# V of the first two batches loaded as two times 72 rows of four tokens, in a fused attention and two-layer feed-forward kernel

## The chip, the cores and the metric

The program runs on one core of one Trainium2 chip. The metric is the device time of one execution in microseconds (us), as the median of several runs. A core has five engines with queues of their own: TensorE (PE, with its weight loads shown apart as PEld), VectorE (DVE), ScalarE (ACT), GpSimd (POOL) and SyncE (SP, which here issues the transfers).

## The reference

`q`, `k`, `v` are (4 batches, 8 heads, 576 tokens, 64). The attention output is the sum of two parts. The *pooled* part averages q, k and v over groups of four tokens (576 becomes 144), does a plain softmax attention on these 144 tokens and repeats each result four times. The *local* part is softmax attention within a band of seven tokens. Both are added, heads and width make 512 columns, 4 x 576 = 2304 rows, and two feed-forward layers follow:

```python
out = out_up + out_local              # (4, 8, 576, 64) -> x (2304, 512)
h = x @ w_in;  g = h * sigmoid(h);  x = g @ w_out        # 512 -> 2048 -> 512
h = x @ w_in2; r = max(h, 0);       out = (s*r*r + b) @ w_out2
```

## The kernel before

**Layers.** Rows are handled in blocks of 512 columns (four blocks, then one of 256). A block of x is kept transposed, 4 tiles of 128 x 512. Each factor of the feed-forward products is split into a high and a low part in a fast format, so that a product is three matmuls (`product`, line 820: high by high, low, and high again with the other half). `mix1` (line 830) goes over 16 slices of the inner width: 4 x 3 matmuls into `hp`, SiLU and a split on ACT and DVE, 4 x 3 matmuls into the four `y` tiles. The second layer does the same from line 930 on. The weights are split on DVE and ACT by `weights` (line 366), at most six slices ahead (`AHEAD`).

**Attention.** Batches 0 and 1 (`NBAND = 2`) do the local part on TensorE (`banded`, line 751); batches 2 and 3 do it on DVE (`local`, line 454). The pooled part is `down` (line 605) for all four; it handles a pair of heads at a time, four pairs a batch. For batches 0 and 1 its inputs come from `rows` (line 565) and `b_turn` (line 698); for batches 2 and 3 from `natural` (line 550).

**V in batches 0 and 1 before the change.** `rows` loads the first 512 tokens of a pair of heads in one transfer into a tile of 128 partitions, each with four consecutive tokens of both heads (line 575). The last 64 tokens of all eight heads come once per batch in a transfer of their own (`zv`, line 583). `pool_rows` (line 592) adds the four tokens of each partition in two DVE steps (lines 595 and 596). `pool_ends` (line 585) sums the last 64 tokens in groups of four with a matmul by a matrix of ones (`pz`, line 589) and copies the 16 rows back. In `down` the 144 pooled tokens are therefore cut in 128 and 16 (`cuts`, line 608): the turned weights `at` are made in these two pieces (line 662) and the value product `pU` (line 680) multiplies, for each head, a piece of 128 rows and then one of 16 rows. Batches 2 and 3 load V as two halves of 72 rows and cut at 72.

**What sets the order.** The kernel is written as a list of operations with a rank (`pr`), estimated costs in microseconds and the buffers that they need. `Weave.plan` (line 121) runs through that list as a simulation: at each step it takes the operation that can start first on any engine, the lowest rank deciding, and writes the instructions out in that order. It also chooses between ACT and DVE for operations marked `EITHER`, and where TensorE would stand idle ahead of the first products it puts in idle matmuls (`spin`, lines 242 and 243). Attention operations on TensorE carry costs multiplied by `slow(ps)` (line 258): 1.25 in batch 0, 1.1 later. Products have rank 100 and above, so any attention operation that is ready goes ahead of them. The plan's estimates set the order only; on the chip each engine takes its instructions in that fixed order and waits where data is late.

Of the kernel before, what the change touches and what calls it, by code (L numbers as in the profile page):

```python
# [16 lines left out]
P = 128  # L17
# [2 lines left out]
SUB = 3  # L20
HALO = 3
WIN = 7
NBAND = 2
NB = 512
GROUPS = [(6, 6, 6), (5, 5, 4, 4)]
GS = 6
QP = 72
# [8 lines left out]
HOLD = {'exp': 0.064, 'silu': 0.785}  # L36
BIAS = 0.306
START = 0.56
FLIGHT = 4
NW = 35  # L40
NACT, NACTV = 0, 1
# [36 lines left out]
class Weave:  # L78
# [42 lines left out]
    def plan(self, pr):  # L121

        ops = self.ops
        need = [len(o[3]) for o in ops]
        ready = [0.0] * len(ops)
        cand, free = {}, {}
        moved, table = 0.0, None
        flight = {"sp": [0.0] * FLIGHT, "act": [0.0] * FLIGHT}
        turns = {k: list(v) for k, v in self.turns.items()}
        slot_of, left, busy, at = {}, {}, set(), {}  # L130
        order, begin, finish, used, placed = [], [0.0] * len(ops), [0.0] * len(ops), [None] * len(ops), [()] * len(ops)

        def avail(bufs):
            t, got = 0.0, []
            for b in bufs:
                if b.slot is None and b not in slot_of:
                    if b.kind in turns and turns[b.kind][0] is not b:
                        return 1e30, got
                    s = min((s for s in self.kinds[b.kind] if s not in busy and all(s is not g for _, g in got)),
                            key=lambda s: at.get(s, 0.0), default=None)  # L140
                    if s is None:
                        return 1e30, got
                    got.append((b, s))
                    t = max(t, at.get(s, 0.0))
            return t, got

        for i, o in enumerate(ops):
            for b in o[4]:
                left[b] = left.get(b, 0) + 1
            for e in o[0]:  # L150
                cand.setdefault(e, [])
                free.setdefault(e, START)
                if not need[i]:
                    cand[e].append(i)
        for _ in ops:
            best = None
            for e, c in cand.items():
                starts = []
                for i in c:
                    t = max(ready[i], free[e])  # L160
                    if e in flight and isinstance(ops[i][1], tuple) and len(ops[i][0]) == 1:
                        t = max(t, flight[e][-FLIGHT] + 0.1)
                    if len(ops[i][0]) > 1:
                        ends = {o: max(ready[i], free[o]) + c for o, c in zip(ops[i][0], ops[i][1])}
                        if (e == "act") != (ends["act"] <= ends["dve"] + BIAS):
                            continue
                    if ops[i][6] and ops[i][6] != table:
                        t = max(t, ready[i] + HOLD[ops[i][6]])
                    t = max(t, avail(ops[i][4])[0])
                    starts.append((t, i))  # L170
                if starts:
                    t0 = min(starts)[0]
                    pick = min((pr[i], i) for t, i in starts if t <= t0 + 1e-9)
                    if best is None or t0 < best[0]:
                        best = (t0, pick[1], e)
            t, i, eng = best
            if t >= 1e30:
                raise RuntimeError("no slot: " + ", ".join(sorted({b.kind for c in cand.values() for j in c for b in ops[j][4] if b.slot is None and b not in slot_of})))
            engs, cost, _, _, bufs, _, need_table = ops[i]
            if len(engs) > 1:  # L180
                cost = cost[engs.index(eng)]
            if need_table and need_table != table:
                table = need_table
                cost += SWITCH
            placed[i] = avail(bufs)[1]
            for b, s in placed[i]:
                slot_of[b] = s
                busy.add(s)
                if b.kind in turns:
                    turns[b.kind].pop(0)  # L190
            order.append(i)
            begin[i], used[i] = t, eng
            if eng in flight and isinstance(cost, tuple):
                parts, move = cost[:2]
                for _ in range(parts):
                    t = max([t, flight[eng][-FLIGHT] + 0.1]) + (cost[2] if len(cost) > 2 else 0.47)
                    moved = max(t + 0.65, moved) + move / parts
                    flight[eng].append(moved)
                free[eng] = t
                end = moved + 0.93  # L200
            else:
                end = free[eng] = t + cost
            finish[i] = end
            for e in engs:
                cand[e].remove(i)
            for j in self.succ[i]:
                need[j] -= 1
                ready[j] = max(ready[j], end + self.lag(eng, ops[j][0]))
                if not need[j]:
                    for e in ops[j][0]:  # L210
                        cand[e].append(j)
            for b in bufs:
                left[b] -= 1
                s = slot_of.get(b, b.slot)
                at[s] = max(at.get(s, 0.0), end + 0.13)
                if not left[b]:
                    busy.discard(s)
        return order, begin, finish, used, placed
# [31 lines left out]
def dve(n, c=1):  # L250
    return c * 0.07 + n / 960.0
# [4 lines left out]


def slow(ps):
    return 1.25 if ps == "ps_first" else 1.1


def pe(n):
    return n / 2400.0 + 0.0134
# [3 lines left out]
def kernel(ctx, tc, q, k, v, w1_in, w1_out, w2_in, w2_out, s2, b2, cst, out):  # L267
# [297 lines left out]
    def rows(b, i, names, pr, kind, after=[], by="sp"):  # L565


        for nm in names:
            t = nat[b, i, nm] = Buf(kind, [P, 2, NT4, D] if nm == "v" else [P, NT4, 2 * D], F32, "n" + nm)

            def load(t=t, nm=nm):
                queue = nc.scalar if by == "act" else nc.sync
                row = (b * H + 2 * i) * S
                if nm == "v":
                    dma(t[:].rearrange("p a r d -> p a (r d)"), bass.AP(tens[nm].tensor, row * D, [[NT4 * D, P], [S * D, 2], [1, NT4 * D]]), queue)
                    return
                for a in range(2):
                    dma(t[:, :, a * D:(a + 1) * D], bass.AP(tens[nm].tensor, (row + a * S) * D, [[D, P], [P * D, NT4], [1, D]]), queue)

            op(by, (1, 0.9, 0.5) if nm == "v" else (2, 1.55, 0.73), load, w=[t], r=after, pr=pr)  # L580
            if (b, nm) not in ends_of:
                z = ends_of[b, nm] = Buf(kind, [NZ, H, D], F32, "z" + nm)
                op("sp", (1, 0.8, 0.73), lambda z=z, nm=nm: dma(z[:], tens[nm][b, :, NT4 * P:, :].rearrange("h s d -> s h d")), w=[z], r=after, pr=pr)
# [8 lines left out]
    def pool_rows(b, i, pr):  # L592

        t = nat[b, i, "v"]
        op("dve", dve(4 * D), lambda: nc.vector.tensor_tensor(out=t[:, :, 0:2], in0=t[:, :, 0:2], in1=t[:, :, 2:4], op=ALU.add), w=[t], pr=pr)
        op("dve", dve(2 * D), lambda: nc.vector.tensor_tensor(out=t[:, :, 0], in0=t[:, :, 0], in1=t[:, :, 1], op=ALU.add), w=[t], pr=pr)

# [7 lines left out]
    def down(b, i, pr, ps="ps"):  # L605
        qd, kd = q_diag[i % 2], Buf("dk", [P, SD], F32, "dk")
        plain = (b, i) in bq
        cuts = [(0, P), (P, SD)] if plain else [(0, QP), (QP, SD)]
        if plain:
            pool_rows(b, i, pr)  # L610
            (q_, qi), (k_, ki) = bq[b, i], bk[b, i]
# [58 lines left out]
            op(EITHER, (act(2 * SD), dve(2 * SD)), lambda eng, kt=kt, pT=pT, n=k1 - k0: copy(eng, at[:n, kt], pT[:]), w=[(at, kt)], r=[pT], pr=pr)  # L670
        up = upT[b]
        pU = Buf(ps, [P, SD], F32, "pU")
        for a in range(2):
            def value(a=a):
                for kt, (k0, k1) in enumerate(cuts):
                    if plain:
                        rows = nat[b, i, "v"][:, a, 0] if kt == 0 else ends_of[b, "v"][:NZ // 4, 2 * i + a]
                    else:
                        rows = sums["v"](kt)[:, a * D:(a + 1) * D]
                    nc.tensor.matmul(pU[a * D:(a + 1) * D], lhsT=rows, rhs=at[:k1 - k0, kt, :, a * DQ:(a + 1) * DQ], start=(kt == 0), stop=(kt == 1))  # L680

            op("pe", 0.33 * slow(ps), value, w=[(pU, a), (up, i)], r=[at, nat[b, i, "v"]] + ([ends_of[b, "v"]] if plain else []), pr=pr)

        def keep(eng):
            if plain:
# [134 lines left out]
    def product(t, n, lhs, rhs, w, r, first, last, pr):  # L820
# [2 lines left out]
            for i in range(3):  # L823
                nc.tensor.matmul(t(), lhsT=lhs(i), rhs=rhs(i), start=(first and i == 0), stop=(last and i == 2))  # L824

        op("pe", 3 * pe(n), fn, w=w, r=r, pr=pr)

    HP, LP = 100.0, 101.0

# [44 lines left out]
        weights(1, 0, DECF, [], RAWF) if m == 0 else weights(1, m, DEC0 + DECS * m, [split_end[1, m - AHEAD]] if m >= AHEAD else [], RAW0 + RATE * m)  # L874
    for hq in A:
        b_turn(0, hq, PT0 + PTS * hq, "ps_first")
        if hq == 0:
            pool_ends(0, PN0, "ps_first")
        down(0, hq, PN0 + PNS * hq, "ps_first")
        for js in runs(first):  # L880
# [10 lines left out]
    for b in range(1, NBAND):  # L891
        lead, rest = list(range(c1 // QB)), list(range(c1 // QB, NJ))
        vr = None
        for hq in A:
            rows(b, hq, "qkv", NAT1 + PT1S * hq, "w", [split_end[1, D1 + D1S * hq]])
            vw = v_load(b, [hq], lead, NAT1 + PT1S * hq, [split_end[1, D1 + D1S * hq]])
            b_turn(b, hq, PT1 + PT1S * hq, "ps")
            if hq == 0:
                pool_ends(b, PT1, "ps")
            down(b, hq, PT1 + PT1S * hq)  # L900
            for js in runs(lead):
# [125 lines left out]
```

## Time and profile before

| what | value |
|---|---|
| median of 3 runs | 928.7 us (928.09 to 930.0) |
| time of the profiled execution | 928.93 us |
| its span, first to last instruction | 927.1 us |
| PE busy | 907.8 us (98%) |
| DVE busy | 594.9 us (64%) |
| ACT busy | 413.7 us (45%) |
| mean granted TensorE clock | 0.993 |

The span and the 1.8 us around it make up the profiled execution. Matmuls are pipelined, and the end of each is modelled; how long a group of them keeps the engine is read from the start of the group to the start of what follows, not from its length in the row.

### The profile page before, as it was taken

How to read it: one execution, taken by the hardware profiler on the slowest of the kernel's cores; microseconds unless marked ns; L12 is line 12 of the kernel's file. 1: busy time of each engine (PE TensorE's matmuls, PEld its weight loads, DVE VectorE, ACT ScalarE, POOL GpSimd, SP SyncE). 2: the span in 40 equal slices, each digit the busy share in tenths (PEclk: the TensorE clock that was granted, in tenths of full speed). 3: DMA queues.
4: the chain of work that ended last, by engine and by line, in shares of the span. 5: the costliest groups of instructions: out<-in, count | busy, mean ns of one | idle time of the engine just before them, and what ended most of it. 6: DMA issues, size and time to landing. Idle time of an engine off the chain costs nothing.

```text
span 927.1 us, 13217 instructions
## 1 busy us (share of the span) xinstructions
PE 907.8 (98%) x5065; PEld 738.9 (80%) x5065; DVE 594.9 (64%) x1137; ACT 413.7 (45%) x911; POOL 0.2 (0%) x4
## 2 busy tenths in 40 slices
PE   8889999999999999999999999999999999999997
PEld 6667777777777877777889988888888888888896
DVE  4999599689999999995139998332232224222332
ACT  4966778667357433342234543332232224222322
POOL 0000000000000000000000000000000000000000
PEclk7999999999999999999999999999999999999999
DMA  9995411445333212220068460020011000100101
GB/s 197 276 270 174 137 46 46 126 122 128 86 111 81 79 65 66 68 74 1 1 208 288 164 227 0 1 91 1 1 46 46 1 1 23 45 1 1 29 18 24
DMA packets 98331, 78.10 MB, mean 84 GB/s; under 512 B 62557, under 2 KB 84443, under 8 KB 98267
## 3 DMA queue, kind: packets, MB, share of 16 engines
q1 hardware_dynamic: 97078, 76.95, 28.7%
q8 instruction: 40, 0.66, 0.3%
q10 hardware_dynamic: 1188, 0.30, 0.2%
q14 instruction: 25, 0.20, 0.1%
HBM read 67.79 MB, written 9.44 MB: 83 GB/s over the span
## 4 chain that ended last, share of the span: by engine, by line
PE 75%; DVE 16%; ACT 4%; DMA 2%; issue 1%; SPq 0%; ACTq 0%; DVEq 0%
PE hp L824 34%; PE o L824 21%; PE y L824 14%; DVE tmp L500 3%; DVE tmp L463 2%; DVE sc L466 2%; DVE tmp L505 2%; DVE gl L845 2%; DVE tmp L506 1%; PE pU L680 1%; PE pS L644 1%; PE pB L765 1%; PE pBO L807 1%; DVE pv L507 1%; DMA zk<-in_k_dram 1%
## 5 line engine op out<-in xcount | busy, mean ns | idle before, releaser
L824 PE MATMUL hp<-xh,wi 128*128 128x512 f32 (+1 forms) x640 | 205.2, 380 | 2.5 <-ACT g L843 2.0
L824 PE MATMUL y<-gh,wo 128*128 128x512 f32 (+1 forms) x640 | 200.7, 376 | 0.0
L824 PE MATMUL hp<-yh,wi 128*128 128x512 f32 (+1 forms) x640 | 185.9, 368 | 0.0
L824 PE MATMUL o<-wo,gh 128*128 128x512 f32 x576 | 177.4, 389 | 0.0
L956 DVE SCALAR_TENSOR_TENSOR gl<-r,sbt,gh 128x512 fp32r<-128x512 f32 (+1 forms) x80 | 55.8, 698 | 151.0 <-ACT gh L954 150.7
L824 PEld LDWEIGHTS hp<-xh,wi 128*128 128x128 f32 x640 | 116.9, 189 | 27.3 <-ACT g L843 5.7
L824 PEld LDWEIGHTS y<-gh,wo 128*128 128x128 f32 x640 | 116.9, 189 | 20.6 <-issue 1.2
L824 PEld LDWEIGHTS hp<-yh,wi 128*128 128x128 f32 x640 | 116.5, 189 | 20.2
L954 ACT ACTIVATE gh<-r,sbt 128x512 fp32r<-128x512 f32 (+1 forms) x80 | 54.6, 683 | 159.5 <-PE o L824 151.1
L824 PEld LDWEIGHTS o<-wo,gh 128*128 128x128 f32 x576 | 107.8, 188 | 22.1
L824 PE MATMUL y<-gl,wo 128*128 128x512 f32 (+1 forms) x320 | 118.3, 370 | 0.0
L824 PE MATMUL hp<-xl,wi 128*128 128x512 f32 (+1 forms) x320 | 118.2, 369 | 0.0
L824 PE MATMUL hp<-yl,wi 128*128 128x512 f32 (+1 forms) x320 | 117.7, 368 | 0.0
L824 PE MATMUL o<-wo,gl 128*128 128x512 f32 x288 | 112.0, 389 | 0.0
L844 ACT CAST gh<-g 128x512 fp32r<-128x512 f32 (+1 forms) x80 | 46.2, 577 | 102.1 <-PE y L824 101.3
L952 DVE SCALAR_TENSOR_TENSOR r<-r,sbt 128x512 f32<-128x512 f32 (+1 forms) x80 | 55.8, 697 | 51.3 <-ACT r L951 51.2
L845 DVE TENSOR_TENSOR gl<-g,gh 128x512 fp32r<-128x512 f32 (+1 forms) x80 | 50.6, 632 | 39.9 <-ACT gh L844 39.5
L951 ACT ACTIVATE r<-hp 128x512 f32<-128x512 f32 (+1 forms) x80 | 44.5, 556 | 63.9 <-DVE gl L956 45.4
L824 PEld LDWEIGHTS hp<-yl,wi 128*128 128x128 f32 x320 | 60.3, 188 | 10.0
L824 PEld LDWEIGHTS y<-gl,wo 128*128 128x128 f32 x320 | 60.5, 189 | 9.3 <-DVE gl L845 0.7
L824 PEld LDWEIGHTS hp<-xl,wi 128*128 128x128 f32 x320 | 60.5, 189 | 7.6
L843 ACT ACTIVATE g<-hp 128x512 f32<-128x512 f32 (+1 forms) x80 | 44.4, 556 | 48.1 <-DVE gl L845 45.2
(134 smaller groups left out, 1007.7 us busy)
## 6 DMA issues: line engine op xcount, KB each, us to landing
wi_raw<-in_moe_w_in_dram SPq DMA_DIRECT2D x32, 512.0 KB
wo_raw<-in_moe_w_out_dram SPq DMA_DIRECT2D x32, 512.0 KB
yd<-ys SPq DMA_DIRECT2D x16, 256.0 KB
yt<-yd SPq DMA_DIRECT2D x4, 1024.0 KB
nq<-in_q_dram SPq DMA_DIRECT2D x16, 144.0 KB
nk<-in_k_dram SPq DMA_DIRECT2D x16, 144.0 KB
lk<-in_k_dram SPq DMA_DIRECT2D x6, 384.0 KB
lv<-in_v_dram SPq DMA_DIRECT2D x6, 384.0 KB
```

The lines of the kernel that those rows point to most:

```text
L463: op("dve", dve(n * WIN * D), lambda t=t, i0=i0, n=n, h2=h2: nc.vector.tensor_tensor(out=t[:], in0=wide(qs[:, h2, i0:i0 + n, :].unsqueeze( ...
L466: op("dve", dve(n * WIN * D), lambda t=t, i0=i0, n=n, h2=h2: nc.vector.tensor_reduce(out=sc[:, h2, i0:i0 + n, :], in_=t[:], axis=AX.X, op= ...
L500: op("dve", dve(n * WIN * D), lambda t=t, i0=i0, n=n, h2=h2: nc.vector.tensor_tensor(out=t[:], in0=wide(e[:, h2 * ns + i0:h2 * ns + i0 + n ...
L505: nc.vector.tensor_tensor(out=t[:, :, 0:3], in0=t[:, :, 0:3], in1=t[:, :, 4:7], op=ALU.add)
L824: nc.tensor.matmul(t(), lhsT=lhs(i), rhs=rhs(i), start=(first and i == 0), stop=(last and i == 2))
L843: op("act", act(n), lambda g=g, hp=hp: nc.scalar.activation(out=g[:], in_=hp[:], func=AF.Silu), w=[g], r=[hp], pr=-5, table="silu")
L844: op("act", act(n), lambda g=g, gh=gh: nc.scalar.copy(out=gh[:], in_=g[:]), w=[gh], r=[g], pr=-5)
L845: op("dve", dve(n), lambda g=g, gh=gh, gl=gl: nc.vector.tensor_tensor(out=gl[:], in0=g[:], in1=gh[:].bitcast(F32), op=ALU.subtract), w=[gl ...
L951: op("act", act(n), lambda r=r, hp=hp: nc.scalar.activation(out=r[:], in_=hp[:], func=AF.Relu), w=[r], r=[hp], pr=-5)
L952: op("dve", dve(n) + 0.07, lambda r=r: nc.vector.scalar_tensor_tensor(out=r[:], in0=r[:], scalar=sbt[:, 0:1], in1=r[:], op0=ALU.mult, op1= ...
L954: op("act", act(n) + 0.1, lambda r=r, gh=gh: nc.scalar.activation(out=gh[:], in_=r[:], func=AF.Identity, bias=sbt[:, 1:2]), w=[gh], r=[r, ...
L956: op("dve", dve(n) + 0.07, lambda r=r, gh=gh, gl=gl: nc.vector.scalar_tensor_tensor(out=gl[:], in0=r[:], scalar=sbt[:, 1:2], in1=gh[:].bit ...
```

## The change

`VQ`, the set of batches that keep the old layout of V, is empty. V of batches 0 and 1 is loaded as two halves of 72 partitions with four tokens each, in two transfers per pair of heads; `zv`, `pz` and its copy are gone, and so is the cut at 128. The pooled sums of a pair now have 72 partitions with twice as many elements. The value product multiplies 72 rows twice. In the plan, attention operations on TensorE outside batch 0 are no longer stretched by 1.1, and each change between products and other work on TensorE costs 0.07 us (`TURN`).

```diff
+VQ = ()
+TURN = 0.07
...
-        moved, table = 0.0, None
+        moved, table, mixing = 0.0, None, False
...
-                    if ops[i][6] and ops[i][6] != table:
+                    if ops[i][6] in HOLD and ops[i][6] != table:
...
-            if need_table and need_table != table:
+            if eng == "act" and need_table and need_table != table:
...
             else:
+                if eng == "pe" and (need_table == "mix") != mixing:
+                    mixing = not mixing
+                    cost += TURN
                 end = free[eng] = t + cost
...
 def slow(ps):
-    return 1.25 if ps == "ps_first" else 1.1
+    return 1.25 if ps == "ps_first" else 1.0
...
         for nm in names:
+            if nm == "v" and b not in VQ:
+                t = nat[b, i, nm] = Buf(kind, [QP, 2, 2, 4, D], F32, "n" + nm)
+
+                def halves(t=t):
+                    for k in range(2):
+                        dma(t[:, k].rearrange("p a r d -> p a (r d)"), bass.AP(tens["v"].tensor, ((b * H + 2 * i) * S + k * 4 * QP) * D, [[4 * D, QP], [S * D, 2], [1, 4 * D]]),
+                            nc.scalar if by == "act" else nc.sync)
+
+                op(by, (2, 1.3, 0.4), halves, w=[t], r=after, pr=pr)
+                continue
...
         t = nat[b, i, "v"]
+        if b not in VQ:
+            op("dve", dve(8 * D), lambda: nc.vector.tensor_tensor(out=t[:, :, :, 0:2], in0=t[:, :, :, 0:2], in1=t[:, :, :, 2:4], op=ALU.add), w=[t], pr=pr)
+            op("dve", dve(4 * D), lambda: nc.vector.tensor_tensor(out=t[:, :, :, 0], in0=t[:, :, :, 0], in1=t[:, :, :, 1], op=ALU.add), w=[t], pr=pr)
+            return
...
-        cuts = [(0, P), (P, SD)] if plain else [(0, QP), (QP, SD)]
+        cuts = [(0, P), (P, SD)] if plain and b in VQ else [(0, QP), (QP, SD)]
...
+        ends = plain and b in VQ
+
+        def value(pairs):
+            for kt, a in pairs:
+                k0, k1 = cuts[kt]
+                if not plain:
+                    rows = sums["v"](kt)[:, a * D:(a + 1) * D]
+                elif not ends:
+                    rows = nat[b, i, "v"][:, kt, a, 0]
+                else:
+                    rows = nat[b, i, "v"][:, a, 0] if kt == 0 else ends_of[b, "v"][:NZ // 4, 2 * i + a]
+                nc.tensor.matmul(pU[a * D:(a + 1) * D], lhsT=rows, rhs=at[:k1 - k0, kt, :, a * DQ:(a + 1) * DQ], start=(kt == 0), stop=(kt == 1))
...
+            for a in range(2):
+                op("pe", 0.33 * slow(ps), partial(value, [(0, a), (1, a)]), w=[(pU, a), (up, i)], r=[at, nat[b, i, "v"]], pr=pr)
...
-        op("pe", 3 * pe(n), fn, w=w, r=r, pr=pr)
+        op("pe", 3 * pe(n), fn, w=w, r=r, pr=pr, table="mix")
...
-        if hq == 0:
+        if hq == 0 and 0 in VQ:
             pool_ends(0, PN0, "ps_first")
...
-            if hq == 0:
+            if hq == 0 and b in VQ:
                 pool_ends(b, PT1, "ps")
```

## Rows read from the trace of the kernel before

**Rows 1.** Busy time by stretch: us, PE, PEld, DVE, ACT, POOL, PEclk, DMA share, GB/s.

```profile
0.00:20.00 20.00, 15.95 (x197) 13.07 (x198) 8.38 (x23) 7.79 (x31) 0.20 (x4) 0.74 1.01 194
20.00:62.00 42.00, 36.52 (x456) 26.81 (x453) 41.35 (x114) 34.39 (x129) 0.00 (x0) 1.00 1.05 288
62.00:200.00 138.00, 137.74 (x909) 102.55 (x907) 114.19 (x287) 102.90 (x258) 0.00 (x0) 1.00 0.42 114
200.00:480.00 280.00, 276.70 (x1307) 220.37 (x1302) 231.86 (x391) 119.75 (x235) 0.00 (x0) 1.00 0.26 74
```

**Rows 2.** Timeline of PE, value products of one pair in batch 1 (start, length).

```profile
105.94 0.46 PE L680 MATMUL pU<-dat,nv 128*64 128x144 f32 x2
106.33 0.45 PE L680 MATMUL pU<-dat,zv 16*64 16x144 f32 x2
...
107.48 0.50 PE L824 MATMUL y<-gh,wo 128*128 128x512 f32 x1
```

**Rows 3.** Timeline of PE, value products of two pairs in batches 2 and 3.

```profile
221.76 0.86 PE L680 MATMUL pU<-dat,nv 72*64 72x144 f32 x8
222.55 0.98 PE L644 MATMUL pS<-dk,q_diag 128*96 128x144 f32 x6
...
234.53 0.72 PE L680 MATMUL pU<-dat,nv 72*64 72x144 f32 x8
235.17 0.50 PE L824 MATMUL hp<-xh,wi 128*128 128x512 f32 x1
```

**Rows 4.** Timeline of PE around the sum of the last tokens in batch 1.

```profile
75.01 0.40 PE L824 MATMUL y<-gl,wo 128*128 128x512 f32 x1
75.24 0.40 PE L824 MATMUL y<-gh,wo 128*128 128x512 f32 x1
75.57 1.03 PE L589 MATMUL pz<-zv,four 64*16 64x512 f32 x2
76.53 0.50 PE L824 MATMUL y<-gh,wo 128*128 128x512 f32 x1
76.87 0.40 PE L824 MATMUL y<-gl,wo 128*128 128x512 f32 x1
```

**Rows 5.** DVE sums of V by line: durations in ns min/median/max, first and last start.

```profile
L595 DVE TENSOR_TENSOR nv<-nv x8: 391/414/426, 12.3 to 155.7; 128x256 f32<-128x256 f32 x8
L596 DVE TENSOR_TENSOR nv<-nv x8: 275/280/285, 13.3 to 156.6; 128x128 f32<-128x128 f32 x8
L601 DVE TENSOR_TENSOR nv<-nv x8: 677/679/687, 187.8 to 297.0; 72x512 f32<-72x512 f32 x8
L602 DVE TENSOR_TENSOR nv<-nv x8: 357/412/420, 188.5 to 299.1; 72x256 f32<-72x256 f32 x8
```

**Rows 6.** Chain that ended last, up to 62 us (start, us, what).

```profile
14.12 1.81 PE pz L589 x2
...
41.20 0.60 DVE wo L394
...
51.61 1.55 PE pU L680 x8
...
61.30 0.74 PE hp L824 x2
```

**Rows 7.** Timeline of DVE in the first 20 us, with the idle time before and its releaser.

```profile
12.26 0.42 DVE L595 TENSOR_TENSOR nv<-nv 128x256 f32<-128x256 f32 x1 [2.74 <-DMA nv<-in_v_dram]
...
15.97 0.68 DVE L318 COPY zv<-pz 16x512 f32<-16x512 f32 x1 [0.43 <-PE pz L589]
```

**Rows 8.** Busy time by stretch of 1 us, columns as in rows 1.

```profile
18.00:19.00 1.00, 1.00 (x6) 0.99 (x6) 1.00 (x4) 0.00 (x0) 0.00 (x0) 0.50 1.18 287
19.00:20.00 1.00, 1.00 (x35) 0.94 (x34) 1.00 (x6) 0.74 (x2) 0.00 (x0) 0.98 1.08 203
```

**Rows 9.** Timeline of SP's queue, the transfers of V of the first pair.

```profile
5.78 0.82 SPq L331 DMA_DIRECT2D nv<-in_v_dram  x1
7.05 0.61 SPq L331 DMA_DIRECT2D zv<-in_v_dram  x1
```

More of the change, by code (lines that the diff above doesn't have):

```diff
@@ L672, in down @@
         pU = Buf(ps, [P, SD], F32, "pU")
[L673 to L682, printed above, removed]
+        ends = plain and b in VQ
[9 more added lines that the diff above has]
+                nc.tensor.matmul(pU[a * D:(a + 1) * D], lhsT=rows, rhs=at[:k1 - k0, kt, :, a * DQ:(a + 1) * DQ], start=(kt == 0), stop=(kt == 1))
+        if ends:
+            op("pe", 1.2 * slow(ps), partial(value, [(0, 0), (0, 1), (1, 0), (1, 1)]), w=[pU, (up, i)], r=[at, nat[b, i, "v"], ends_of[b, "v"]], pr=pr)
+        else:
+            for a in range(2):
+                op("pe", 0.33 * slow(ps), partial(value, [(0, a), (1, a)]), w=[(pU, a), (up, i)], r=[at, nat[b, i, "v"]], pr=pr)
         def keep(eng):
```

## The prediction

> **What bounds the kernel now.** I read the busy time by stretch first, then the timeline of TensorE where the edited operations run, the chain that ended last in the opening stretch, and at last the timelines of VectorE and of SP's queue. The first view splits the run [rows 1]. Up to 20 us the kernel waits for its first transfers: PE is busy 15.95 us (idle matmuls included), DVE only 8.38. From 20 to 62 us DVE has no time left (41.35 of 42) and PE has (36.52 of 42): batch 0's attention and the first weight splits share DVE. From 62 us on PE decides: busy 137.74 of 138 and then 276.70 of 280, so all its idle time up to 480 us is 0.26 + 3.30 = 3.6 us. There a microsecond of PE work removed is a microsecond of time; before 62 us it need not be. After 480 us the second layer runs, which the edits don't touch.
>
> **Value products, batch 1.** Four matmuls (two passes each) make `pU` of a pair. With 128 and 16 rows they start at 105.94 and the next work at 107.48 [rows 2]: 1.54 us. The alternation is dear: the 16-row product starts 0.39 us after the 128-row one. The three other pairs of batch 1 show the same steps. Batches 2 and 3 do the same product with 72 rows twice, in 235.17 - 234.53 = 0.64 us, once in 222.55 - 221.76 = 0.79 [rows 3]. The changed kernel issues just that form, so 0.75 to 0.90 us go per pair; I take 0.90, as three of the four pairs that I looked at in batches 2 and 3 take 0.64 or 0.65. Four pairs: -3.6 us (bounds -3.0 to -3.6), all on PE while it is the bound.
>
> **The sum of the last tokens, batch 1.** `pz` holds PE from 75.57 to 76.53, 0.96 us. It is a visit between products as well: those follow one another by 0.23 us (75.01 to 75.24), but 0.33 pass up to `pz` and 0.34 after the first product behind it [rows 4], so a visit costs 0.10 + 0.11 more. Together -1.17 us; should the plan put other attention work into that place, the 0.21 stays: bounds -0.96 to -1.17. Its copy there runs on ACT, which has slack (102.90 of 138) [rows 1]; nothing for it.
>
> **The sums of V on DVE.** Before, a pair costs 414 + 280 ns; as 72 rows with twice the elements 679 + 412 ns [rows 5]. That is +0.40 us a pair, for eight pairs +3.2 us. In batch 1 the cover is DVE's slack, 114.19 of 138 [rows 1]: nothing, at worst +1.6 if that slack is gone when the pair is due. In batch 0 there is no cover after 20 us.
> The row shows more elements per partition in place of more partitions, and the time following the elements. The Trainium skill's page "Trainium Kernel Development and Optimization", under Best Practices, says to tile to 128 partitions always; that speaks against this edit. By it, with all 3.2 us on the path, the sum below would end at about 925.1 in place of 923.5.
>
> **The opening, batch 0.** Four terms. (a) `pz` takes 1.81 us on the chain at 14.12 [rows 6], at half the clock, and DVE waits 0.43 us for it and copies for 0.68 [rows 7]. With both gone the next transposes of PE and DVE's work come forward; as ACT's exponentials of the first pair are late next, I take DVE's part, -1.1 us (bounds 0 to -1.8). (b) The first pair's longer sum, +0.40, ahead of the first band mask: its data was already what DVE waited for (2.74 us) [rows 7]. (c) The other three pairs' sums on a full DVE: +1.2. (d) Value products 0.90 cheaper in four pairs: one of these groups lies on the chain, at 51.61 [rows 6]; -0.9 for it, the rest is hidden behind DVE (bound -3.6). Sum: -1.1 + 0.4 + 1.2 - 0.9 = -0.4 us, with bounds of -1.8 - 3.6 = -5.4 (DVE's additions covered by weight splits that nobody waits for yet) and 0.4 + 1.2 = +1.6.
>
> **Transfers.** Per pair two transfers of V in place of one, and no `zv`: SP issues 8 more and 2 fewer. One issue holds SP for 0.82 or 0.61 us in the opening [rows 9]. For the first pair the second half takes about the place of `zv`, so whatever is queued behind stays where it was; the bytes are the same in all. Later pairs push what is behind them in SP's queue (q and k of the next pair, weights) back by one issue each, at most 0.8 us; PE waits for none of these after 62 us. Zero, bounds 0 to +0.8 on the way to the first product. The cut at 72 changes the rows of the turned weights, not their number or their columns: zero.
>
> **The new plan.** `TURN` and the factor of 1.0 change no instruction, but every start time that the plan computes, hence the order on all engines and the choice of ACT or DVE. No row shows the result. Best case: the waits after 62 us vanish, -3.6; as bound above I take the same amount again, +3.6 [rows 1]. A visit counted with its real cost should put waits in the right place, reshuffled ranks may do the opposite: zero.
>
> **Sum.** -3.6 - 1.2 - 0.4 + 0 = -5.2 us. Against the profiled execution, 928.93 us (span 927.1 and 1.8 around it), that is 923.7; this execution lies 0.2 above the median, so the median becomes **923.5 us**.
>
> **Rivals.**
> *The opening gains in full* (0.16). The chain in the opening changes engine many times, and DVE's time between 20 and 62 us is partly weight splits that PE needs much later; if the plan puts the sums in front of these, the -5.4 of the opening is had in place of -0.4: 918.5. Against it: DVE's stretch is as good as full [rows 1].
> *The new order gives most of it back* (0.13). After 62 us the waits double by 3.6: 923.5 + 3.6 = 927.1. For it: the fixed ranks stay as they were while every computed time moves. Against it: waits are few today and the costs of the plan come nearer to the rows (0.33 us per half of a value product is what rows 3 show).
> *DVE sets the opening, slower* (0.13). Place: DVE's queue between 20 and 62 us. The longer sums, planned ahead of x's last pieces, let the plan move weight splits in front of attention work. A split of a tile has three steps of 0.60 (lines 387, 390 and 394; one stands in [rows 6]), 1.8 us. PE then starts its unbroken products later, and that is never regained. Beyond 5.2 / 1.8 = 2.9 tiles the gain is eaten; four tiles give 923.5 + 7.2 = 930.7. For it: 41.35 of 42. Against it: the work added there is only 1.6 us, less the 0.68 of the copy. The rule on 128 partitions cited above points the same way.
> *The dear step isn't due to the 16 rows* (0.03). Were it the alternation of the two heads' output halves, it would stay: only `pz` and the opening would count, 928.7 - 1.2 - 0.4 = 927.1. Against it: the 72-row groups alternate these halves as well [rows 3].
> *The clock rises late* (0.03). TensorE runs at 0.50 through 18 to 19 us and at full rate (2.4 GHz) from 19 to 20 on, after a stretch with PE busy [rows 8]. Without `pz` PE may stand idle ahead of it. Half of the time spent at the low level is lost, so it takes some 14 us more at 0.50 to lose 7: 930.5.
>
> **How the numbers follow.** The forecast itself has 0.52, with 921.5 to 926 as its own range. A measurement of this kernel tells 0.2%, about 1.9 us, from no change: below 926.8 is faster, above 930.6 slower. Faster: 0.52 + 0.16 + 0.04 (a mild form of the second rival) = 0.72. Same: 0.09 of the second rival, 0.02 of the third, 0.03 of the fourth = 0.14. Slower: 0.11 of the third, 0.03 of the last = 0.14. The range 918.5 to 930 leaves out half of the first rival (0.08), half of the third (0.06) and the last (0.03).
>
> **What would show it.** Right: `pU` groups of batch 1 that last 0.64 to 0.80 us from start to next start, no `pz`, sums of V on DVE at 0.68 and 0.41, the unbroken products, which begin at 61.30 on the chain [rows 6], within a microsecond of that, and the stretch from there to the second layer some 4.8 us shorter. Wrong: an unbroken stream that starts more than 2 us later (third rival) or 3 us earlier (first), PE idle time beyond 6 us between 62 and 480 (second), steps of 0.39 in `pU` (fourth), or 0.50 in the clock column after 20 us (last).

## The result, and the profile after

The changed kernel takes 934.47 us (median of 4 runs, 933.07 to 936.11), the kernel before 928.39 beside it: a ratio of 1.0065 [1.005, 1.0081], 6.1 us slower. Forecast were 923.5 us and a range up to 930. The profiled execution, the fastest of the four, took 933.07 us (span 931.1, PE busy 907.2, DVE 598.9, ACT 402.6, mean clock 0.995), 4.1 more than the one of before.

Busy time by stretch, changed kernel, columns as in [rows 1]:

```profile
0.00:20.00 20.00, 16.91 (x280) 15.33 (x282) 10.91 (x31) 9.78 (x40) 0.20 (x4) 0.91 1.05 205
20.00:62.00 42.00, 36.69 (x490) 27.86 (x486) 41.69 (x110) 31.39 (x111) 0.00 (x0) 1.00 1.07 287
62.00:200.00 138.00, 134.02 (x893) 99.94 (x894) 121.77 (x298) 93.03 (x239) 0.00 (x0) 0.99 0.43 117
200.00:480.00 280.00, 275.01 (x1292) 218.85 (x1291) 222.26 (x385) 119.61 (x228) 0.00 (x0) 1.00 0.23 67
```

The reader is to see PE's third and fourth row: idle time is now 3.98 + 4.99 = 9.0 us, where it was 3.6 [rows 1]. At the same time ACT lost 9.9 us of work between 62 and 200 us and DVE gained 7.6: the plan also shares the copies out differently.

The value products of a pair in batch 1, timeline of PE, changed kernel:

```profile
107.04 0.40 PE L851 MATMUL y<-gh,wo 128*128 128x512 f32 x1
107.36 0.72 PE L703 MATMUL pU<-dat,nv 72*64 72x144 f32 x8
108.01 0.98 PE L663 MATMUL pS<-dk,q_diag 128*96 128x144 f32 x6
108.73 0.49 PE L851 MATMUL y<-gh,wo 128*128 128x512 f32 x1
```

The group, four matmuls of two passes each, keeps PE for 108.01 - 107.36 = 0.65 us; it was 1.54 [rows 2]. No `pz` is left. The sums of V on DVE, by line (ns min/median/max, first and last start), cost what 72 rows cost in the other batches [rows 5], and the first one starts 1.0 us sooner than before [rows 7]:

```profile
L611 DVE TENSOR_TENSOR nv<-nv x8: 657/681/689, 11.3 to 151.6; 72x512 f32<-72x512 f32 x8
...
L612 DVE TENSOR_TENSOR nv<-nv x8: 395/414/421, 12.4 to 152.9; 72x256 f32<-72x256 f32 x8
```

So the work went, and the time came back, about half of it as waits. What PE waits for between 62 and 480 us, first in the kernel before (us in total, times, longest), then the longest in the changed one. `pt` turns the local results `pv` of batches 2 and 3, `g` is SiLU's result, `gl` its low part, `dat` the turned weights of `pU`, `dk` the pooled keys:

```profile
PE pt L515 <- DVE pv L507: 2.0, 6, 0.6
PE pt L515 <- DVE sm L489: 0.6, 1, 0.6
PE hp L824 <- ACT g L843: 0.3, 1, 0.3
...
```

```profile
PE hp L851 <- ACT g L870: 2.7, 3, 2.0
PE pt L520 <- DVE pv L512: 2.1, 5, 0.9
PE pU L703 <- ACT dat L323: 1.0, 3, 0.5
PE y L851 <- DVE gl L872: 0.8, 2, 0.6
PE pS L663 <- DVE dk L634: 0.4, 1, 0.4
...
```

In all that view has 3.3 us in 10 waits before and 8.7 us in 21 waits after, on many tiles and none of them large except one. That one ends the opening. The chain that ended last shows who was late there (start, us, what; L389 and L399 are steps of a weight split), and the busy time by 1 us what followed:

```profile
60.69 0.68 DVE wo L399
61.37 0.14 DVE be L800
61.51 0.33 DVE f L389
61.84 0.17 DVE wi L399
62.01 0.35 issue
62.37 0.69 DVE gl L872
...
63.14 0.61 ACT g L870
...
63.79 0.50 PE hp L851
```

```profile
64.00:65.00 1.00, 1.00 (x5) 0.82 (x5) 1.00 (x2) 0.78 (x2) 0.00 (x0) 0.98 0.90 146
65.00:66.00 1.00, 1.00 (x4) 0.71 (x4) 1.00 (x3) 0.84 (x2) 0.00 (x0) 0.50 0.93 158
66.00:67.00 1.00, 1.00 (x4) 0.81 (x3) 1.00 (x3) 0.00 (x0) 0.00 (x0) 0.50 1.09 184
67.00:68.00 1.00, 1.00 (x4) 0.81 (x3) 1.00 (x4) 0.95 (x2) 0.00 (x0) 0.50 1.15 263
68.00:69.00 1.00, 1.00 (x5) 0.79 (x5) 1.00 (x3) 0.99 (x2) 0.00 (x0) 0.81 1.01 208
```

PE stood idle for 2.03 us ahead of 63.79, and from 65.0 on its clock was granted at 0.50 (1.2 of 2.4 GHz) for 3.4 us: the clock column adds up to 0.02 + 3 x 0.50 + 0.19 = 1.7 us lost.

**The account of the 9.3 us between forecast (-5.2) and profile (+4.1).** From the start of each PE instruction to the next, idle time apart: the opening ends at 63.79 in place of 61.30 [rows 6], but 36 product matmuls stand before that point, not 24; at 0.23 us each that is 2.49 - 2.76 = -0.3, near the -0.4 forecast. From there to the last `y` matmul of the first layer (528.88 before, 531.33 after) PE takes 467.5 us both times, where -4.8 from the layout and -2.8 for the products already done would have left 460.0. The 7.5 us are 3.8 of idle time, 1.7 of the clock, 1.4 of longer steps at the attention's matmuls (those of the banded local part `pBT`, `pB` and `pBO` +1.7, the others together -0.3) and 0.6 in the products. The last 1.5 us come in the second layer, 0.45 of it idle time (0.3 a wait on `gl`), the rest mostly three product matmuls more that stand behind the last `y`. That is 0.1 + 7.5 + 1.5 = 9.1; the 0.2 left are rounding and the time around the span.

### The profile page after: what moved, and what is told of

Read it like the earlier page. It is cut to its first block, busy times and chain, and to the rows that moved or that the text cites. A ratio compares the mean times of both kernels' runs of the same rounds, so it can differ in the third digit from the quotient of the medians.

```text
span 931.1 us, 13426 instructions
## 1 busy us (share of the span) xinstructions
PE 907.2 (97%) x5171; PEld 740.4 (80%) x5171; DVE 598.9 (64%) x1153; ACT 402.6 (43%) x878; POOL 0.2 (0%) x4
## 4 chain that ended last, share of the span: by engine, by line
PE 64%; DVE 24%; DMA 4%; ACT 4%; issue 3%; SPq 1%; DVEq 0%; ACTq 0%
PE hp L851 30%; PE o L851 20%; PE y L851 11%; DVE tmp L505 3%; DVE tmp L468 3%; DVE sc L471 3%; DVE gl L872 2%; DMA vw<-in_v_dram 2%; DVE tmp L510 2%; SPq L336 1%; DVE tmp L511 1%; DVE f L392 1%; DMA yd<-ys 1%; DVE f L395 1%; DMA nq<-in_q_dram 1%
```

## The experiments

The theory: the layout brings what was forecast, and the plan's new costs lose more than that, by putting PE's work in an order that waits. The rivals: the layout is itself slower (the opening, DVE's longer sums), or the clock is what was lost; later on, that the charge hurts by its place, by the length that it gives the plan, or by leaving no slack for late data.

Two numbers of the plan were changed with the layout: the **charge** at each change between products and other work (`TURN`), and the **factor** on attention's costs on PE outside batch 0. Medians are in us; the kernel before took 928.4 to 929.05 beside them. PE's idle time is 415.5 less its busy time in the stretch 64.5 to 480 us, so that the wait at the end of the opening is not in it.

| kernel | V | charge | factor | median (runs) | ratio to before | PE idle |
|---|---|---|---|---|---|---|
| before | old | 0 | 1.1 | 928.39 | 1 | 3.6 |
| after | new | 0.07 | 1.0 | 934.47 (4) | 1.0065 [1.005, 1.0081] | 7.2 |
| order_kept | new | order of before | | 929.04 (12) | 1.0001 [0.999, 1.0011] | 5.9 |
| kept_warm | new | order of before | | 928.25 (11) | 0.9998 [0.9988, 1.0008] | 6.1 |
| v_only | new | 0 | 1.1 | 927.02 (11) | 0.998 [0.9971, 0.9989] | 5.3 |
| plan_only | old | 0.07 | 1.0 | 935.17 (5) | 1.0066 [1.0054, 1.0078] | 7.1 |
| b1_only | new in batch 1 | 0.07 | 1.0 | 938.29 (4) | 1.0096 [1.0083, 1.0109] | 9.8 |
| v_turn | new | 0.07 | 1.1 | 935.62 (5) | 1.0078 [1.0066, 1.009] | 8.0 |
| v_half | new | 0.035 | 1.0 | 925.02 (5) | 0.9959 [0.9946, 0.9972] | 5.9 |
| v_slow | new | 0 | 1.0 | 923.58 (5) | 0.9949 [0.9937, 0.9961] | 3.2 |
| v_fast | new | 0 | 0.8 | 924.35 (11) | 0.9962 [0.9951, 0.9972] | 3.5 |
| v_att | new | 0 | 1.3 | 932.63 (7) | 1.0037 [1.0023, 1.0051] | 8.9 |
| slow_only | old | 0 | 1.0 | 928.68 (11) | 0.9999 [0.9989, 1.0009] | 3.6 |
| after_lag | new | 0.07 | 1.0 | 935.63 (6) | 1.008 [1.0057, 1.0103] | 8.5 |
| vslow_lag | new | 0 | 1.0 | 923.81 (5) | 0.995 [0.9937, 0.9962] | 2.0 |
| turn_even | new | 0.07, products cheaper | 1.0 | 923.11 (5) | 0.9944 [0.993, 0.9957] | 2.9 |
| all_slow | new | 0.07, DVE and ACT dearer | 1.0 | 923.01 (5) | 0.9936 [0.9924, 0.9949] | 4.0 |

### Layout and plan taken apart

**order_kept** is the kernel before with V in the new layout. The operations for the last tokens stay in the plan and issue nothing, so every engine keeps its order of before; nothing of the result is left out.

```diff
...
-        op("pe", 1.0, lambda: nc.tensor.matmul(pz[:], lhsT=four1[:NZ], rhs=z[:].rearrange("p h d -> p (h d)")), w=[pz], r=[z, four1], pr=pr)
+        op("pe", 1.0, lambda: None, w=[pz], r=[z, four1], pr=pr)
...
-        cuts = [(0, P), (P, SD)] if plain else [(0, QP), (QP, SD)]
+        cuts = [(0, QP), (QP, SD)]
...
-                        rows = nat[b, i, "v"][:, a, 0] if kt == 0 else ends_of[b, "v"][:NZ // 4, 2 * i + a]
+                        rows = nat[b, i, "v"][:, kt, a, 0]
```

> The new V layout (two halves of 72 rows, no last-token sum, value products of 72 rows) with the order of before: the plan sees the costs and buffers of before, and the operations of the last tokens stay in it with nothing to issue. Theory A (the instructions save what the prediction said, the new order of the plan loses it): 921 to 925 us, value products of batch 1 at 0.64 to 0.80 us a pair, idle time of TensorE between 62 and 480 us near the 3.6 of before. Rival B (the longer sums on VectorE and the extra transfers cost it, wherever they stand): 930 to 936 us, with the unbroken products starting later than 61.3 us.

**v_only** is the changed kernel with both numbers of the plan as before, **plan_only** the kernel before with both new numbers, **b1_only** the changed kernel with the old layout in batch 0.

```diff
-TURN = 0.07
+TURN = 0.0
...
-    return 1.25 if ps == "ps_first" else 1.0
+    return 1.25 if ps == "ps_first" else 1.1
```

> The new V layout, planned with the costs of before (no cost for a change of kind, attention work stretched by 1.1). Theory A1 (any new order loses, since the ranks are fixed): 930 to 936 us. Theory A2 (the new costs in the plan are at fault): 921 to 926 us. Rival B (the layout itself): 932 to 937 us.

```diff
+TURN = 0.07
...
+                if eng == "pe" and (need_table == "mix") != mixing:
+                    mixing = not mixing
+                    cost += TURN
...
-    return 1.25 if ps == "ps_first" else 1.1
+    return 1.25 if ps == "ps_first" else 1.0
...
```

> The V layout of before, planned with the cost of 0.07 us for a change of kind and the factor of 1.0. Theory A1 (any new order loses): 930 to 937 us. Theory A2 (the new costs are at fault): 934 to 940 us, about 6 us plus the 5 that the layout saves above before. Rival B (the layout itself): 927 to 930 us, as before.

```diff
-VQ = ()
+VQ = (0,)
```

> The changed kernel with the old V layout in batch 0 alone (there the four value products of a pair stand in one operation, those of 128 rows first). If the loss is made in batch 0's opening: 924 to 929 us. If it is made by the order of the mixed stretch after 62 us: 931 to 937 us.

The two numbers of the plan, on the layout of before, cost 0.66% or 6.3 us by themselves (plan_only), as much as the whole change. The layout without them gains only 1.9 us (v_only), with both of them 0.7 (the changed kernel less plan_only), and in the order of before nothing (order_kept). b1_only is the slowest of all, though its batch 1 has the cheap value products: what moves these times is the order, and its loss can't be read as a price of batch 0's layout. Only plan_only fell where a theory put it, and it fell into the ranges of two: order_kept and v_only lie in none of their ranges, and b1_only lies 1.3 us above its second one.

Its windows show in part why order_kept gains nothing. Busy time of order_kept between 30 and 60 us, columns as in [rows 1]:

```profile
32.00:33.00 1.00, 0.41 (x3) 0.32 (x4) 1.00 (x5) 0.89 (x3) 0.00 (x0) 1.00 1.13 230
33.00:43.00 10.00, 10.00 (x80) 8.00 (x81) 9.60 (x29) 8.39 (x35) 0.00 (x0) 0.51 1.09 254
...
53.00:60.00 7.00, 7.00 (x50) 5.00 (x50) 5.60 (x12) 2.06 (x5) 0.00 (x0) 0.54 1.08 341
```

PE is busy for 0.41 of the microsecond from 32 to 33, and then works at half the clock, 17 us in all; 19 product matmuls are begun by 62 us, where before had 27. After that PE waits 5.6 us in 13 waits, where before waits 3.3. Eight product matmuls at 0.23 us and 2.3 us more of waits are 4.1 of the 4.8 us that the layout was to bring. **kept_warm** is order_kept with idle matmuls where batch 0 lost its work, to part these two.

```diff
...
-        op("pe", 1.0, lambda: None, w=[pz], r=[z, four1], pr=pr)
+        op("pe", 1.0, lambda: fill(30) if ps == "ps_first" else None, w=[pz], r=[z, four1], pr=pr)
...
+                if ps == "ps_first":
+                    fill(10)
```

> The kernel with the new V layout in the order of before, and idle matmuls on TensorE in the opening, 30 in the place of the first batch's sum of last tokens and 10 after each head's value product, about as long as what the layout took away there. If the gain of the layout was lost because TensorE had less to do in the opening and its clock fell to 0.50 for 17 us: no fall between 25 and 62 us, some 27 products started by 62 us as before, and 926 to 928 us against 929.0 without them. If the clock is not the reason: 928.5 to 930.5 us.

Its profile shows one fall of the clock, 3.4 us long, and 24 product matmuls by 62 us, but the time is only 0.8 us lower than order_kept's and the intervals overlap; 928.25 lies between the two ranges that were expected. The clock in the opening is at most a small part; the waits stayed (7.3 us in 15). turn_even (below) says the same: its clock is 0.53 from 39 to 50 us, where v_slow's is 1.00, and it is as fast as v_slow.

### Which of the two numbers

**v_turn** puts the factor back to 1.1, **v_slow** takes the charge away, **v_fast** also sets the factor to 0.8, **v_half** halves the charge.

```diff
-    return 1.25 if ps == "ps_first" else 1.0
+    return 1.25 if ps == "ps_first" else 1.1
```

> The new V layout with one of the two new plan costs: 0.07 us for a change of kind, attention work still stretched by 1.1. Theory C (a plan that takes TensorE for slower than its rows say puts TensorE's operations where the results of VectorE and ScalarE come just in time, and TensorE waits; a plan that takes it for faster leaves slack): this is the slowest TensorE of all plans, so 934 to 939 us, idle time of TensorE between 62 and 480 us 7 us or more. Rival D (each new order lands anywhere, no trend): 926 to 937 us, no relation to the others.

```diff
-TURN = 0.07
+TURN = 0.0
```

> The new V layout with the other new plan cost: no cost for a change of kind, attention work stretched by 1.0 in place of 1.1. Theory C: TensorE is taken for faster than in the plan that gave 927.0, so 924 to 927.5 us. If the factor of 1.0 is the culprit: 931 to 935 us. Rival D: 926 to 937 us.

```diff
-TURN = 0.07
+TURN = 0.0
...
-    return 1.25 if ps == "ps_first" else 1.0
+    return 1.25 if ps == "ps_first" else 0.8
```

> The new V layout, no cost for a change of kind, attention work of the later batches shrunk to 0.8 in the plan, well under its rows. Theory C: 922 to 926.5 us, idle time of TensorE between 62 and 480 us under 5 us. Rival E (a plan nearer to the rows is better, and the changed plan lost for another reason): 930 us or more. Rival D: 926 to 937 us.

```diff
-TURN = 0.07
+TURN = 0.035
```

> The changed kernel with half the cost for a change of kind, 0.035 us; its plan ends at 915.4 us of its own count, between those that gave 923.6 (908.6) and 934.5 (923.9). Theory C, and rival F as well: 926 to 931 us. Rival D (no trend, each order by luck): outside of that, most likely over 931 or under 926.

Taking the charge out is enough to undo the loss: without it the changed kernel takes 923.58 us, the forecast's 923.5 and 0.4 under the range expected. Half of the charge costs 1.4 us, the whole of it 10.9; v_half's 925.02 lies under 926, where it was said to speak for the rival that each order lands by luck: the loss does not grow evenly with the charge. v_slow between 62 and 480 us, busy time of two stretches and what PE waited for:

```profile
62.00:200.00 138.00, 136.84 (x923) 104.18 (x923) 123.37 (x303) 92.34 (x245) 0.00 (x0) 1.00 0.44 119
200.00:480.00 280.00, 277.49 (x1329) 223.17 (x1328) 226.64 (x387) 124.61 (x238) 0.00 (x0) 1.00 0.27 78
```

```profile
PE pt L520 <- DVE pv L512: 0.8, 4, 0.3
PE hp L851 <- ACT g L870: 0.8, 1, 0.8
PE y L851 <- DVE gl L872: 0.7, 1, 0.7
PE pt L520 <- DVE sm L494: 0.4, 1, 0.4
...
```

Idle time is 1.16 + 2.51 = 3.7 us, as before the change; `pt` waits 1.2 us in place of 2.3 and no `pU` waits. Its last `y` of the first layer starts at 521.94, the changed kernel's 9.4 us later, and by the account of PE's steps over the whole time up to it these 9.4 are 4.0 of idle time, 3.7 in the products (1.7 of it the clock) and 1.7 at attention's own steps.

### What the charge does: its place, its length, or PE's pace

Charging 0.07 us at each change is not wrong as a price: in the kernel before, a step from a product into other work takes 0.289 us against 0.236 between products. So why does it hurt? **v_att** makes PE slow in the plan without any charge, by the factor alone. **slow_only** sets the factor to 1.0 on the old layout, to have the layout by itself at the plan costs of v_slow.

```diff
-TURN = 0.07
+TURN = 0.0
...
-    return 1.25 if ps == "ps_first" else 1.0
+    return 1.25 if ps == "ps_first" else 1.3
```

> The new V layout, no cost for a change of kind, attention work of the later batches stretched by 1.3 in the plan: the plan ends at 924.4 us of its own count, as the changed kernel's does (923.9), without any charge at a change. Theory C (what loses is a plan that takes TensorE for slow, whatever makes it slow): 932 to 937 us. Rival F (the charge at the changes is what loses): 923 to 928 us, as with factors of 0.8 to 1.1.

```diff
-    return 1.25 if ps == "ps_first" else 1.1
+    return 1.25 if ps == "ps_first" else 1.0
```

> The V layout of before, no cost for a change of kind, attention work at 1.0 in place of 1.1. Beside the 923.6 us of the new layout with the same plan costs this prices the layout: if it is worth the 4.8 us predicted after 62 us and nothing in the opening, 927.5 to 929.5 us; if it is worth only the 1.9 us that it gave at a factor of 1.1, 924.5 to 926.5 us.

Stretching attention does much the same as the charge (932.63 us, 8.9 us idle): the place where the plan loses PE's time is not what matters. And at these plan costs the layout is worth 928.68 - 923.58 = 5.1 us, or 4.6 by the two ratios: the size that was forecast for it. That holds at this pair of numbers only; at the others the layout brought 1.9, 0.7 and 0 us (above), so how much of it is kept depends on the order.

**after_lag** and **vslow_lag** count the results of other engines 0.4 us later for PE, from 62 us of the plan on, so that no order rests on data that is ready just in time.

```diff
-                ready[j] = max(ready[j], end + self.lag(eng, ops[j][0]))
+                ready[j] = max(ready[j], end + self.lag(eng, ops[j][0]) + (0.4 if end > 62.0 and eng != "pe" and ops[j][0] == ("pe",) else 0.0))
```

> The changed kernel with both new plan costs, and one more edit in the plan: from 62 us of its own count on, a result of another engine counts as ready for TensorE 0.4 us later, so the plan puts TensorE's attention work and products that much behind it. Its plan ends at 928.2 us of its own count (changed kernel: 923.9). If TensorE loses because results come just in time: idle time of TensorE between 62 and 480 us falls from 7.2 to 5 us or less, and the time is 928 to 932 us. If the loss goes with the length of the plan for another reason: 935 to 939 us, idle time as before or more.

> The kernel that gave 923.6 us (no charge for a change of kind, attention work at 1.0) with the 0.4 us by which results of other engines count as ready later for TensorE from 62 us on. If that slack is harmless by itself: 922.5 to 926 us. If it costs by itself, which would explain that it didn't help the changed kernel: 928 to 932 us.

A fixed slack mends nothing (935.63, PE idle 8.5 us; the 7.2 in its expectation are those from 64.5 us on) and harms nothing (923.81). That data comes just too late, by a few tenths, is not borne out as the reason.

**turn_even** keeps the charge and takes the same time off the products, so that PE's pace over the plan is v_slow's again (the 450th product operation is planned at 422.6 us; 421.2 in v_slow, 436.6 in the changed kernel). **all_slow** keeps the charge and makes DVE and ACT slower in the plan too.

```diff
 def pe(n):
-    return n / 2400.0 + 0.0134
+    return n / 2400.0 + 0.002
```

> The changed kernel with its charge of 0.07 us for a change of kind, and 0.0114 us less for each matmul of a product in the plan, so that the first layer's products are planned on the whole where the plan without a charge has them (product operation 450 at 422.6 us; 421.2 without a charge, 436.6 in the changed kernel). If TensorE's pace as a whole decides: 922 to 927 us, idle time of TensorE between 62 and 480 us 3 to 5 us. If the charge at the changes itself does it (rival F): 930 to 935 us, idle time 6 us or more.

```diff
             if need_table and need_table != table:
                 table = need_table
                 cost += SWITCH
+            if eng in ("dve", "act") and not isinstance(cost, tuple):
+                cost *= 1.05
```

> The changed kernel's plan with the costs of VectorE and ScalarE raised by 5% as well; its plan ends at 927.8 us of its own count (changed kernel: 923.9). If what counts is TensorE's pace in the plan against that of the other two: the order becomes much like that of the plan without a charge, 924 to 929 us. If a longer plan loses whatever makes it longer: 935 to 940 us.

Both give the whole loss back: 923.11 and 923.01 us, the second 1 us under its range. Stretch from 64.5 to 480 us, columns as in [rows 1], of the changed kernel, turn_even and all_slow:

```profile
64.50:480.00 415.50, 408.32 (x2182) 318.18 (x2181) 341.54 (x678) 211.41 (x464) 0.00 (x0) 1.00 0.30 83
```

```profile
64.50:480.00 415.50, 412.57 (x2245) 327.99 (x2245) 344.32 (x671) 222.76 (x499) 0.00 (x0) 1.00 0.32 90
```

```profile
64.50:480.00 415.50, 411.55 (x2227) 323.30 (x2228) 343.17 (x667) 214.01 (x491) 0.00 (x0) 1.00 0.32 90
```

turn_even has the charge at every change: the charge by itself does no harm here. all_slow's plan ends at 927.8 us, as late as v_turn's (928.7): nor does a long plan. What v_slow, turn_even and all_slow share, and the changed kernel lacks, is PE's pace in the plan beside that of DVE and ACT. The other plans fit: the 450th product operation is planned to end at 413 to 428 us in all kernels of 923 to 929 us, old layout or new, and at 436 to 442 in all of 932 to 938; all_slow alone has 439.7, with DVE and ACT 5% slower as well. The loss sets in between 428 (v_half) and 436 (plan_only); why there, no run shows. After 64.5 us what PE still waits for in turn_even are four groups, 5.5 us less the 2.7 of the opening's end, with no `pt`:

```profile
PE hp L851 <- ACT g L870: 3.4, 3, 2.7
PE y L851 <- DVE gl L872: 1.4, 2, 1.2
PE pT L686 <- ACT qkT L323: 0.5, 1, 0.5
PE pT L686 <- DVE xf L530: 0.2, 1, 0.2
```

**What stays open.** The plan puts an attention operation in front of the products as soon as its data is there by the plan. If PE is slow in the plan, it finds more data there than the chip has when PE comes to it. That is argued, not shown: which single placements cost the time was not traced, and the traces bear it out only in part. Of the 1116 matmul records of attention, 1054 stand ahead of the 750th product matmul in v_slow and all_slow and 1040 in turn_even, but 1078 in the changed kernel, v_turn and plan_only and 1061 in v_att; yet after_lag has 1058, and b1_only, the slowest, 1054. A truer plan is not a better one either: at the 150th product operation the chip stands some 1.3 us behind the plan in the changed kernel, 6.5 in v_slow and 15.8 in v_fast, and the last two are the fast ones. More than half of the loss against v_slow is not idle time but longer steps, of which only the 1.7 us of the clock have a cause. The spread between orders remains too: v_only and v_slow differ by 3.4 us for a factor of 1.1 or 1.0 that does nothing on the old layout (slow_only).

**A kernel faster than both** is the new layout with v_slow's plan, or turn_even's or all_slow's: 923.0 to 923.6 us, 0.5 to 0.6% under the kernel before.

## Why the prediction was wrong

**The step that failed** is the term "The new plan", put at zero with bounds of 3.6 either way. The two numbers cost 7.5 us on the new layout (934.47 less v_only's 927.02) and 6.3 on the old one (plan_only). The bound was taken from the idle time of before, "the same amount again", and nothing ties what a new order can lose to what the old one loses: idle time between 62 and 480 us grew from 3.6 to 9.0 us, 2.0 of that at the end of the opening, and 3.7 us more came as longer steps and a clock fall that no wait shows. The sentence that a visit counted with its real cost "should put waits in the right place" was wrong in kind: the charge changed PE's pace beside DVE and ACT, and that, not the place of the visits, made the loss (v_att, turn_even). The charge alone cost 10.9 us (the changed kernel less v_slow); the factor did nothing on the old layout (slow_only, 0.9999) and gained 3.4 us on the new one (v_slow against v_only).

The term also left out that the layout changes the plan by itself: it takes operations out and gives others new costs. With both numbers of before, -5.2 was forecast and -1.9 came (v_only); -1.9 + 7.5 = +5.6 is nearly the whole of the +6.1. That v_slow's 923.58 us meets the forecast of 923.5 is therefore in part luck: of the four pairs of kernels that differ by the layout, one shows its full worth.

**Value products, batch 1**: right. Its four groups took 6.2 us and now 2.8, three of 0.65 and one of 0.88: -3.4; with those of batches 2 and 3 it is -3.6. The steps of 0.39 us from matmul to matmul went with the 16-row pieces, while a 72-row group steps by 0.65 / 4 = 0.16: the fourth rival falls. This row is where the Trainium skill's page "TensorEngine Tiling (Array Packing)", under Key Properties, bears: a change of the tiling mode drains TensorE. The alternation of 128 x 64 and 16 x 64 [rows 2] agrees with it, though no run separates the drain from the size of the pieces.

**The last tokens' sum, batch 1**: right in that 0.96 us of `pz` are gone; what its visit cost beside was not to be seen apart.

**The sums of V on DVE**: right, 0.68 and 0.41 us. The rule of tiling to 128 partitions always, which the prediction cites from the Trainium skill's page "Trainium Kernel Development and Optimization", under Best Practices, is not borne out here: in four pairs of kernels with equal plan numbers or equal order the 72 rows are 5.1, 1.9, 0.7 and 0 us faster.

**The opening**: -0.3 for -0.4, but made of other things. On PE `pz` (1.8 us), `pU` (6.2 to 4.3) and `pq` (6.6 to 5.1) gave 5.2 us; 3.9 of these went to idle matmuls (8.2 to 12.1), and products came in earlier. Of the 0.90 us a pair that (d) took over from batch 1, about half came: a pair's group takes 0.97 to 1.10 us there, not 0.65. DVE was full as forecast (41.69 of 42).

**Transfers**: zero or a little better; DVE's wait of 2.74 us for the first V [rows 7] is 0.3 now.

**Rivals.** "The new order gives most of it back" had the mechanism, its waits after 62 us, and its sign that they exceed 6 us is there with 9.0; its price of +3.6 was a third of what came. "DVE sets the opening, slower" had its sign too, a stream that starts 2.5 us late behind a weight split (60.69 to 63.79 above), yet 12 more product matmuls had been done by then, and only the clock fall behind it, 1.7 us, was lost. "The opening gains in full" did not come: the stream begins 2.5 us later, not 3 earlier. "The clock rises late" did not happen; it fell again at 65.0, which the prediction's last sign names but its rival does not price. The sign that the stretch to the second layer is some 4.8 us shorter is not there (467.5 us both times): the layout's terms came on PE, and the order took them.

## What to carry to other kernels

Where a planner orders the queues, time a change of its costs by itself before it goes in beside a change of the work: here a charge of 0.07 us turned a gain of 5 us into a loss of 6, and the same layout was worth anything from 0 to 5 us by the order that it was run in. Costs of one engine in such a plan are not good by being true alone; keep the pace of the engines beside each other, and if one gets a new charge, take the same time off its other costs or add to the others' and measure both. And bound a change of order by what orders of this kernel have been seen to differ by (here some 15 us between 923 and 938, the layouts of V included), not by the idle time that is left.

## What the runs showed that was not expected

TensorE's clock falls in the middle of the opening, not only at the start: with the same order and less work it was granted at 0.51 from 33 to 43 us and at 0.54 from 53 to 60 (order_kept, above), after PE had been idle from 31 to 32 and busy for 0.41 of a microsecond between 32 and 33. The changed kernel's fall at 65.0 us follows 2.03 us of idle time. Such a fall need not cost anything where PE has time: turn_even, v_half and v_fast are granted 0.50 from about 40 to 50 us, v_slow and all_slow 1.00, and turn_even (923.11 us) is as fast as these two (923.58 and 923.01). That half of the time at the low level is lost, as the prediction's last rival has it, did not hold in that stretch.

The scatter of one program mostly goes with the mean granted clock: the four runs of the changed kernel have 933.07, 934.48, 934.46 and 936.11 us at 0.995, 0.990, 0.988 and 0.987; order_kept's twelve lie from 926.7 at 0.990 to 931.69 at 0.985 (all_slow's five don't follow it: 920.97 at 0.993, 923.96 at 0.995). It does not explain the differences between the kernels: plan_only's five runs lie at 0.992 to 0.994 with 934.8 to 936.09 us, where runs of the kernel before at 0.993 take about 929.
